# The square that the Newton step of a layer norm reads: from SBUF to PSUM, in a kernel whose order of work is a table

## The chip, the cores and the metric

The kernel runs on one core of a Trainium2 chip. Five engines of the core matter here, each with its own queue that it works through in order: TensorE (PE in the rows, with its weight loads as PEld), VectorE (DVE), ScalarE (ACT), GpSimd (POOL) and SyncE (SP, which here only starts transfers). The metric is the device time of one launch in microseconds (us): 888.38 us as the median of three runs (888.12 to 890.67).

## The reference

```python
# dynamic convolution: 7 taps, weights by token and head (softmax over the taps)
w = exp(weight_gen - max(weight_gen, -1)); w = w / (sum(w, -1) + 1e-9)     # (8, 4224, 8, 7)
y[b, s, h*24:(h+1)*24] = sum_k w[b, s, h, k] * x_pad[b, s + k, h*24:(h+1)*24]   # x: (8, 4224, 192)
# layer norm without a bias, two products with a relu between them, and the residual
xn = (y - mean(y)) / sqrt(var(y) + 1e-6) * g_ln
out = y + maximum(xn @ w_ch1, 0) @ w_ch2            # w_ch1: 192 x 768, w_ch2: 768 x 192
```

## The kernel before, in words

The 8 x 4224 tokens lie as 128 partitions of 264 tokens each. They are worked in 25 parts: three of 4 tokens per partition, twenty of 12, one of 8 and one of 4. A part's way through the engines:

- SP loads `x` into a ring and the tap weights `w`. The softmax goes over DVE (maximum L453, sum L469), POOL (L455, L473) and ACT; ACT writes the normalised tap weights of a chunk of 6 tokens into one of two PSUM banks, `wn` (L485).
- DVE multiplies `x` by the tap weights for seven taps, in four instructions per chunk (L522: three of 128x2304 into `pr` and one of 128x1152 into `y`). The products are added into `y` by POOL (L525) and by transfers that add, started from POOL (L528).
- ACT takes the mean and the variance of every token (L586, L591). Then follows, once per part, the reciprocal root for all of its tokens at once: on ACT `root` (a logarithm L613, an exponential L614 and the square of the result L615, all on rows of `s4` in SBUF), and on DVE `newton` (L618, twice L620, L622), four small instructions that sharpen the root by one Newton step. `newton` keeps two of its intermediate rows in the spare columns of a `wn` bank (`aux`), the bank that the last multiplication before it read.
- ACT scales the tokens (`xh`, L634) and rounds them to a high half in f16 (L703), POOL makes the low half (L705), and a transposing transfer puts both into `xT`. The first two groups of 4 tokens are transposed on TensorE instead (L657), and DVE makes their low half (`tlo`, L669).
- For each group of 4 tokens TensorE runs three units of the first product (L727, 36 instructions with weights loaded for each, into one of two `ph` buffers) and, for the group before, two halves of the second product (`p0`, `p1`, L778, 72 instructions each, into the single buffer `po`). A `ph` is evicted by ACT (relu to f16, `hh`, L742) and then by DVE (the rest that f16 lost, `hlo`, L744); `po` is scaled and added to `y` by DVE (L830), and SP writes `y` out.

The weights are prepared on the chip in the first 60 us, and four transfers swap halves of the first weight (`c_w`, L991) before the first unit can run through.

What sets the order: `PLACE` is a table that gives every operation a number; operations are recorded in the order of these numbers, and so each engine's queue has its order from them. Which buffer an operation gets follows from the same numbers. The semaphore waits are laid on afterwards, from the data and the buffers that two engines share.

Of the kernel before, what the change touches and what calls it, by code (L numbers as in the profile page):

```python
# [32 lines left out]
HALF = 512  # L33
# [4 lines left out]
    'wload': (2, 0, 19, 39, 47, 95, 111, 219, 239, 496, 460, 650, 902, 907, 911, 980, 1122, 1214, 1272, 1651, 1652,  # L38
        1484, 1705),
    'load': (3, 5, 1, 4, 7, 12, 62, 96, 160, 159, 94, 235, 320, 286, 417, 297, 369, 463, 499, 605, 707, 555, 758,  # L40
        798, 941, 843, 878, 914, 1126, 1053, 1211, 1175, 1338, 1174, 1295, 1380, 1379, 1449, 1634, 1576, 1571, 1797,
        1853, 1841, 1773, 1908, 1951, 2065, 2172),
    'w_load': (40, 28, 27),
    'w_gain': (50, 11, 45),
    'w_load2': (41,),
    'w_as': (87,),
    'w_av': (92, 103, 106),
    'w_an': (109,),
    'w_cs': (70,),
    'w_cv': (74, 75, 78),  # L50
    'w_cn': (82,),
    'w_s1': (113, 117, 121, 126, 129),
    'w_d': (154, 137),
    'w_h': (145, 131),
    'w_l': (156, 138),
    'w_lc': (168, 150),
    'w_m': (176, 172, 180, 179),
    'w_c2s': (81, 142, 135),
    'w_c2v': (84, 86, 88, 148, 152, 155, 140, 143, 146),
    'w_c2n': (112, 162, 151),  # L60
    'w_s2': (164, 174, 182, 186, 209, 207, 216, 227),
    'max': (8, 6, 51, 89, 100, 295, 188, 391, 443, 564, 679, 685, 923, 924, 1100, 1109, 1193, 1306, 1373, 1675,
        1686, 1624, 1826),
    'sub': (10, 9, 54, 98, 127, 299, 197, 400, 513, 588, 731, 805, 929, 999, 1104, 1209, 1285, 1409, 1502, 1678,
        1701, 1790, 1960),
    'exp': (13, 14, 65, 105, 171, 311, 230, 426, 527, 607, 738, 853, 931, 1044, 1110, 1222, 1289, 1423, 1516, 1683,
        1716, 1803, 2002),
    'sum': (15, 17, 76, 108, 217, 316, 233, 471, 557, 697, 752, 861, 977, 1059, 1150, 1231, 1292, 1427, 1553, 1695,
        1720, 1886, 2014),
    'log': (16, 23, 90, 114, 229, 319, 395, 483, 580, 730, 781, 882, 1006, 1085, 1206, 1253, 1381, 1450, 1606, 1710,  # L70
        1801, 1913, 2043),
    'less': (18, 26, 93, 122, 264, 363, 431, 524, 585, 735, 801, 892, 1023, 1090, 1226, 1296, 1383, 1468, 1621,
        1713, 1888, 1933, 2045),
    'expw': (20, 21, 38, 43, 107, 99, 187, 169, 284, 282, 371, 390, 470, 457, 569, 570, 646, 660, 765, 767, 865,
        863, 963, 934, 1029, 1058, 1167, 1188, 1274, 1236, 1390, 1347, 1495, 1451, 1590, 1546, 1674, 1687, 1774, 1757,
        1894, 1927, 1969, 1980, 2100, 2076, 2161),
    'keep': (24, 22, 67),
    'c0': (25, 29, 60, 61, 110, 175, 193, 246, 321, 344, 404, 425, 509, 533, 574, 648, 690, 739, 792, 849, 875, 912,
        979, 1027, 1062, 1082, 1185, 1196, 1282, 1374, 1392, 1485, 1531, 1493, 1593, 1667, 1714, 1754, 1810, 1872, 1914,
        1958, 2000, 2041, 2127, 2101, 2194),  # L80
    'c1': (33, 37, 46, 69, 132, 158, 240, 203, 331, 296, 459, 414, 476, 548, 573, 615, 701, 760, 804, 836, 896, 932,
        990, 1050, 1093, 1134, 1197, 1239, 1301, 1342, 1442, 1408, 1524, 1541, 1645, 1655, 1692, 1741, 1849, 1868, 1902,
        1972, 2009, 2070, 2131, 2119, 2193),
    'c2': (32, 36, 42, 49, 128, 153, 211, 263, 298, 362, 374, 437, 508, 485, 610, 593, 674, 732, 814, 770, 867, 952,
        1007, 1001, 1124, 1114, 1219, 1246, 1327, 1348, 1419, 1474, 1512, 1568, 1602, 1639, 1737, 1693, 1844, 1822,
        1946, 1928, 2024, 1985, 2136, 2152, 2181),
# [996 lines left out]
```

## Time and profile before

| | |
|---|---|
| median of three runs | 888.38 us |
| the profiled execution | 893.53 us, of which its span (first to last instruction) 891.8 us |
| mean granted TensorE clock | 0.977 |
| busy: TensorE / DVE / POOL / ACT | 831.6 / 768.1 / 697.2 / 686.7 us |
| `newton`'s first instruction (L618), all 25 | 38.1 us |

How to read it: engine busy time is a share of the span, and an engine that is idle costs only where something later waits for it. The rows below are from the profiled execution alone, which is 5.15 us above the median of the runs that were timed. A row of a timeline gives the start, the length, the instruction, and in brackets how long the engine had stood idle before it and which instruction released it.

### The profile page before, as it was taken

How to read it: one execution, taken by the hardware profiler on the slowest of the kernel's cores; microseconds unless marked ns; L12 is line 12 of the kernel's file. 1: busy time of each engine (PE TensorE's matmuls, PEld its weight loads, DVE VectorE, ACT ScalarE, POOL GpSimd, SP SyncE). 2: the span in 40 equal slices, each digit the busy share in tenths (PEclk: the TensorE clock that was granted, in tenths of full speed). 3: DMA queues.
4: the chain of work that ended last, by engine and by line, in shares of the span. 5: the costliest groups of instructions: out<-in, count | busy, mean ns of one | idle time of the engine just before them, and what ended most of it. 6: DMA issues, size and time to landing. Idle time of an engine off the chain costs nothing. (4 is left out here: it accounts for less than half of the span.)

```text
span 891.8 us, 37250 instructions
## 1 busy us (share of the span) xinstructions
PE 831.6 (93%) x16687; PEld 811.5 (91%) x16687; DVE 768.1 (86%) x646; ACT 686.7 (77%) x1797; POOL 697.2 (78%) x385
## 2 busy tenths in 40 slices
PE   5557999999899999999999998989998989999998
PEld 5347999999899999999999998989998989999997
DVE  6999999999999989999998898999898987874433
ACT  3888899798797887996888968876885869868621
POOL 4898899999889989978988879887886868874100
PEclk9869999999999999999999999999998999999999
DMA  8778687888697997886878887697896756554332
GB/s 237 182 169 173 137 186 168 189 175 164 151 183 154 236 205 151 165 191 147 187 187 183 164 158 160 137 180 145 196 183 124 133 119 136 134 114 96 74 65 81
DMA packets 132157, 140.86 MB, mean 158 GB/s; under 512 B 104102, under 2 KB 106030, under 8 KB 131998
## 3 DMA queue, kind: packets, MB, share of 16 engines
q1 hardware_dynamic: 119326, 88.16, 44.1%
q0 software_dynamic: 12672, 50.34, 29.0%
q8 instruction: 130, 2.13, 1.0%
q14 instruction: 29, 0.24, 0.1%
HBM read 36.43 MB, written 25.95 MB: 70 GB/s over the span
## 5 line engine op out<-in xcount | busy, mean ns | idle before, releaser
L525 POOL TENSOR_TENSOR y<-y,pr 128x1152 f32<-128x1152 f32 (+1 forms) x176 | 469.5, 2675 | 38.0 <-DVE pr L522 17.4
L727 PE MATMUL ph<-xT,c_w 64*128 64x256 f16 x7128 | 420.8, 271 | 20.9 <-DVE hlo L744 14.5
L727 PEld LDWEIGHTS <-c_w 64*128 64x128 f16 x7128 | 388.2, 95 | 29.3 <-issue 23.9
L778 PE MATMUL po<-c_w2h,hh 64*128 64x192 f16 x3120 | 391.8, 244 | 12.6 <-DVE y L830 10.5
L778 PE MATMUL po<-c_w2h,hlo 64*128 64x192 f16 x3120 | 391.6, 244 | 0.1
L778 PE MATMUL po<-c_w2l,hh 64*128 64x192 f16 x3120 | 391.6, 244 | 0.0
L522 DVE TENSOR_TENSOR pr<-x,wn 128x2304 f32<-128x2304 f32 (+2 forms) x138 | 332.2, 2417 | 6.6 <-POOL y L525 2.4
L778 PEld LDWEIGHTS <-hh 64*128 64x128 f16 x6240 | 318.8, 95 | 15.5 <-issue 13.8
L744 DVE SCALAR_TENSOR_TENSOR hlo<-ph,hh 128x1024 f16<-128x1024 f32 x198 | 239.1, 1218 | 86.1 <-ACT hh L742 85.7
L742 ACT ACTIVATE hh<-ph 128x1024 f16<-128x1024 f32 x198 | 199.0, 1012 | 102.6 <-PE ph L727 83.9
L778 PEld LDWEIGHTS <-hlo 64*128 64x128 f16 x3120 | 187.3, 95 | 0.3 <-issue 0.3
L634 ACT ACTIVATE xh<-y,s 128x192 f32<-128x192 f32 x264 | 126.6, 536 | 33.9 <-DVE s L622 31.6
L705 POOL TENSOR_TENSOR hl<-xh,hl 128x768 f16<-128x768 f32 x64 | 109.1, 1714 | 49.9 <-ACT hl L703 34.9
L591 ACT ACTIVATE junk<-y,s 128x192 f32<-128x192 f32 x264 | 119.4, 452 | 9.4 <-PE po L778 3.0
L528 POOL DMA_DIRECT2D pr<-pr x88 | 80.9, 961 | 53.0 <-DVE pr L522 30.2
L586 ACT ACTIVATE junk<-y 128x192 f32<-128x192 f32 x264 | 95.0, 360 | 20.0 <-POOL y L525 9.1
L830 DVE SCALAR_TENSOR_TENSOR y<-po,c_fs,y 128x768 f32<-128x768 f32 (+1 forms) x86 | 68.7, 813 | 4.0 <-PE po L778 4.0
L522 DVE TENSOR_TENSOR y<-x,wn 128x1152 f32<-128x1152 f32 (+2 forms) x47 | 59.5, 1268 | 2.2 <-ACT wn L485 2.2
L703 ACT ACTIVATE hl<-xh 128x768 f16<-128x768 f32 x64 | 53.2, 835 | 2.1 <-PE po L778 1.5
L586 ACT ACTIVATION_READ_ACCUMULATOR junk<-y 128x1 f32 x264 | 49.5, 187 | 0.0
L591 ACT ACTIVATION_READ_ACCUMULATOR junk<-y,s 128x1 f32 x264 | 49.5, 187 | 0.0
L618 DVE SCALAR_TENSOR_TENSOR wn<-s 128x12 f32<-128x12 f32 (+2 forms) x25 | 38.1, 1523 | 8.6 <-ACT s L615 8.3
(77 smaller groups left out, 319.0 us busy)
## 6 DMA issues: line engine op xcount, KB each, us to landing
pr<-pr POOLq DMA_DIRECT2D x80, 576.0 KB, 6.6
x<-in_x_dram SPq DMA_DIRECT2D x40, 576.0 KB, 6.1
out_dram<-y SPq DMA_DIRECT2D x40, 576.0 KB, 5.6
w<-in_weight_gen_dram SPq DMA_DIRECT2D x21, 336.0 KB, 5.8
pr<-pr POOLq DMA_DIRECT2D x8, 384.0 KB, 5.1
x<-in_x_dram SPq DMA_DIRECT2D x5, 384.0 KB, 5.2
out_dram<-y SPq DMA_DIRECT2D x4, 384.0 KB, 4.5
x<-in_moe_w_ch_dram SPq DMA_DIRECT2D x1, 1152.0 KB, 13.0
```

The costliest lines, as they stand in the source:

```text
L522: E.tensor_tensor(out=ov, in0=xv, in1=wv, op=ALU.mult)
L525: Q.tensor_tensor(out=flat(0), in0=flat(0), in1=flat(k), op=ALU.add)
L528: return Q.dma_start(flat(to), flat(k), accum_op=ALU.add, max_dma_last_dim=CHUNK * D * 4)
L586: A.activation(junk, at(y)[:, j, :], AF.Identity, scale=-SQ / D, accum_out=at(s4)[:, 3, t : t + 1])
L591: A.activation(junk, at(y)[:, j, :], AF.Square, scale=SQ, bias=at(s4)[:, 3, t : t + 1], accum_out=at(s4)[:, 0, t : t + 1])
L634: A.activation(paired(xh, t), at(y)[:, i, :].rearrange("p (c q) -> p c q", q=P // 2), AF.Identity, bias=at(s4)[:, 3, g + t : g + t + 1], s ...
L705: lambda xh=xh, hl=hl: Q.tensor_tensor(out=halves(hl, True), in0=pairs(xh), in1=halves(hl, False), op=ALU.subtract),
L727: T_.matmul(ph[:, r, v * 2 * P : (v + 1) * 2 * P], W["w1"][rows, WB[r][c], w, f : f + P], xv[rows, a, c, :, :], start=(v == 0 and k == 0), ...
L742: lambda: A.activation(at(hh)[:, us, :], at(ph), AF.Relu), [ph], [(hh, u)])
L744: lambda: V.scalar_tensor_tensor(out=at(hlo)[:, us, :], in0=at(ph), scalar=0.0, in1=at(hh)[:, us, :], op0=ALU.max, op1=ALU.subtract),
L778: made.append(T_.matmul(at(po)[:, z, e * D : (e + 1) * D], token(b, 2 * z + e, j)[rows], W[w][rows, j, :], start=(ph == 0 and e == 0 and k ...
L830: V.scalar_tensor_tensor(out=ysl, in0=at(po)[:, zs[0] : zs[-1] + 1, : 2 * D], scalar=W["fs"][:, 0:1], in1=ysl, op0=ALU.mult, op1=ALU.add)
```

## The change

ACT's `root` writes the square of the root into a third spare row of the `wn` bank (PSUM) in place of a row of `s4` (SBUF), and `newton`'s first instruction reads it there. So that instruction has one input in SBUF (the variance, `row(0)`) and one in PSUM. The bank is fixed when `root` is recorded, in `mine`. Both operations name a common key, `"aux"`, so that the `root` of a part is placed after the `newton` of the part before. The numbers of `PLACE` are new for all operations; two lines of the table show it. Because of three added lines, a line of this part of the code has a number higher by 3 in the changed kernel: `root`'s square is L618 there, and `newton` L621, L623 and L625.

```diff
 PLACE = {
-    'newton': (97, 141, 183, 258, 358, 466, 559, 664, 757, 855, 961, 1073, 1160, 1279, 1384, 1472, 1580, 1681, 1802,
+    'newton': (97, 159, 190, 254, 362, 464, 564, 669, 757, 857, 961, 1076, 1161, 1282, 1383, 1473, 1581, 1679, 1800,
...
-    assert AUX + 2 * PMAX <= HALF
+    assert AUX + 3 * PMAX <= HALF
...
         def aux(i):
-            return plan.pools["wn"][bank[0]][:, AUX + i * PMAX : AUX + i * PMAX + n]
+            return plan.pools["wn"][mine[0]][:, AUX + i * PMAX : AUX + i * PMAX + n]
+
+        mine = [0]
 
         def root():
+            mine[0] = bank[0]
             A.activation(row(1), row(0), AF.Ln, bias=bias[:, 0:1])
             A.activation(row(1), row(1), AF.Exp, scale=-0.5)
-            A.activation(row(2), row(1), AF.Square)
+            A.activation(aux(2), row(1), AF.Square)
 
         def newton():
-            V.scalar_tensor_tensor(out=aux(0), in0=row(0), scalar=EPS, in1=row(2), op0=ALU.add, op1=ALU.mult)
+            V.scalar_tensor_tensor(out=aux(0), in0=row(0), scalar=EPS, in1=aux(2), op0=ALU.add, op1=ALU.mult)
...
-        op("ACT", 670, ("rstd", S0), root, vs, [(s4, "r")])
-        op("V", 780, ("newton", S0), newton, [*vs, (s4, "r")], [(s4, "n"), *ms])
+        op("ACT", 670, ("rstd", S0), root, vs, [(s4, "r"), "aux"])
+        op("V", 780, ("newton", S0), newton, [*vs, (s4, "r"), "aux"], [(s4, "n"), *ms])
```

What the new table does to the queues is shown at three places. The first is DVE's queue around the twentieth `newton` of the program's twenty-five (the one at 668.51 us in the trace of before); the row that reads `po_106` is the addition of the second product (L830 before, L833 after), the `hlo` rows are evictions. In before:

```order
L744 SCALAR_TENSOR_TENSOR hlo_90<-ph_105,hh_88 128x1024 [waits Activation_49]
L744 SCALAR_TENSOR_TENSOR hlo_90<-ph_104,hh_88 128x1024 [waits Activation_49]
L469 TENSOR_REDUCE sm_94<-w_66 128x96
L618 SCALAR_TENSOR_TENSOR wn_103<-s_99 128x12 [waits DVE_49,Activation_49]
L620 SCALAR_TENSOR_TENSOR wn_103<-wn_103,s_99 128x12 [waits DVE_49]
L620 SCALAR_TENSOR_TENSOR s_99<-wn_103,s_99 128x12 [waits DVE_49]
L622 SCALAR_TENSOR_TENSOR s_99<-wn_103,s_99 128x12
L830 SCALAR_TENSOR_TENSOR y_74<-po_106,c_fs,y_74 128x768 [waits PE_49]
```

And in the change:

```order
L747 SCALAR_TENSOR_TENSOR hlo_90<-ph_104,hh_88 128x1024 [waits Activation_49]
L747 SCALAR_TENSOR_TENSOR hlo_90<-ph_105,hh_88 128x1024 [waits Activation_49]
L469 TENSOR_REDUCE sm_94<-w_66 128x96
L833 SCALAR_TENSOR_TENSOR y_72<-po_106,c_fs,y_72 128x768 [waits PE_49]
L621 SCALAR_TENSOR_TENSOR wn_103<-s_99,wn_103 128x12 [waits Activation_49]
L623 SCALAR_TENSOR_TENSOR wn_103<-wn_103,s_99 128x12 [waits DVE_49]
L623 SCALAR_TENSOR_TENSOR s_99<-wn_103,s_99 128x12 [waits DVE_49]
L625 SCALAR_TENSOR_TENSOR s_99<-wn_103,s_99 128x12
```

The first Newton instruction now names `wn_103` among its inputs, and the addition of the second product moved ahead of `newton`. Elsewhere on DVE most operations keep their rank among DVE's or move by one.

The second place is ACT's queue around the twentieth `root`: the logarithm, the exponential and the square, then the scaling `xh` that waits for DVE's `newton`, the tap weights `wn` of a later chunk, and evictions `hh`. In before:

```order
L591 ACTIVATE junk_101,s_99<-y_75,s_99 128x192 [waits Activation_49] x2
L613 ACTIVATE s_99<-s_99,bias 128x12 [waits Activation_49]
L614 ACTIVATE s_99<-s_99 128x12 [waits Activation_49]
L615 ACTIVATE s_99<-s_99 128x12 [waits Activation_49]
L634 ACTIVATE xh_81<-y_72,s_99 128x3x64 [waits DVE_49,Pool_49]
L634 ACTIVATE xh_81<-y_72,s_99 128x3x64
L485 ACTIVATE wn_102<-e_96 128x336 [waits Pool_49]
L742 ACTIVATE hh_89<-ph_104 128x1024 [waits PE_49]
```

And in the change:

```order
L591 ACTIVATE junk_101,s_99<-y_74,s_99 128x192 [waits Activation_49] x2
L616 ACTIVATE s_99<-s_99,bias 128x12 [waits Activation_49]
L617 ACTIVATE s_99<-s_99 128x12 [waits Activation_49]
L618 ACTIVATE wn_103<-s_99 128x12 [waits DVE_49,Activation_49]
L485 ACTIVATE wn_102<-e_97 128x336 [waits Pool_49]
L637 ACTIVATE xh_82<-y_68,s_99 128x3x64 [waits DVE_49]
L637 ACTIVATE xh_82<-y_68,s_99 128x3x64
L745 ACTIVATE hh_89<-ph_105 128x1024 [waits PE_49]
```

The square has a new wait for DVE, for the multiplication before it that read the bank; 20 of the 25 squares have it. `wn` moved ahead of `xh`.

The third place is DVE's queue at the start, ahead of the first eviction: `xT_85` and `xT_86` are the low halves of the first two groups (`tlo`, L669 before, L672 after), which the first units of TensorE need, and the 128x2304 rows are multiplications. In before:

```order
L522 TENSOR_TENSOR pr_80<-x,wn_102 128x2304 [waits DMAHW5_49,Pool_49]
L522 TENSOR_TENSOR pr_76<-x,wn_102 128x2304 [waits Activation_49]
L927 TENSOR_SCALAR c_r_126<-po_106 128x1 [waits PE_49]
L522 TENSOR_TENSOR pr_77<-x,wn_102 128x2304 [waits DMASW2_49,Pool_49]
L618 SCALAR_TENSOR_TENSOR wn_102<-s_100 128x4 [waits DVE_49,Activation_49]
...
L453 TENSOR_REDUCE mx_93<-w_65 128x96 [waits DMAHW6_49]
L669 TENSOR_TENSOR xT_85<-ph_104,xT_85 128x2x384
L522 TENSOR_TENSOR pr_78<-x,wn_102 128x2304 [waits DMAHW0_49,Activation_49]
L669 TENSOR_TENSOR xT_86<-ph_105,xT_86 128x2x384 [waits Activation_49]
```

And in the change:

```order
L672 TENSOR_TENSOR xT_85<-ph_104,xT_85 128x2x384 [waits PE_49]
L522 TENSOR_TENSOR pr_80<-x,wn_102 128x2304 [waits DMAHW3_49,Pool_49]
L522 TENSOR_TENSOR pr_78<-x,wn_102 128x2304 [waits Activation_49]
L522 TENSOR_TENSOR pr_76<-x,wn_102 128x2304 [waits DMASW2_49,Pool_49]
L930 TENSOR_SCALAR c_r_126<-po_106 128x1 [waits PE_49]
L453 TENSOR_REDUCE mx_93<-w_65 128x96 [waits DMAHW6_49]
L621 SCALAR_TENSOR_TENSOR wn_102<-s_100,wn_102 128x4 [waits Activation_49]
L623 SCALAR_TENSOR_TENSOR wn_102<-wn_102,s_100 128x4 [waits DVE_49]
L623 SCALAR_TENSOR_TENSOR s_100<-wn_102,s_100 128x4 [waits DVE_49]
L625 SCALAR_TENSOR_TENSOR s_100<-wn_102,s_100 128x4
L672 TENSOR_TENSOR xT_86<-ph_104,xT_86 128x2x384 [waits PE_49]
```

The low half of the first group moved ahead of three multiplications, a maximum and a `newton`. TensorE's own queue has the same order of units and halves as before.

## Rows read from the trace of the kernel before

**Rows 1.** The page's first part: busy us, share, instructions by engine.
```profile
PE 831.6 (93%) x16687; PEld 811.5 (91%) x16687; DVE 768.1 (86%) x646; ACT 686.7 (77%) x1797; POOL 697.2 (78%) x385
```
**Rows 2.** Windows: stretch, length, busy by engine (PE to POOL), clock, DMA share, GB/s.
```profile
100.00:150.00 50.00, 48.51 (x1034) 48.18 (x1030) 49.52 (x38) 44.12 (x121) 47.85 (x27) 1.00 0.77 168
800.00:850.00 50.00, 50.00 (x1062) 49.84 (x1058) 21.94 (x28) 35.45 (x84) 16.50 (x10) 1.00 0.38 86
```
**Rows 3.** Timeline of PE, rows with an idle time: start, length, what, [idle <-releaser].
```profile
61.33 6.65 PE L727 MATMUL ph<-xT,c_w 64*128 64x256 f16 x72 [5.44 <-DVE xT L669]
...
89.98 3.37 PE L727 MATMUL ph<-xT,c_w 64*128 64x256 f16 x34 [3.51 <-DVE hlo L744]
...
231.36 0.26 PE L778 MATMUL po<-c_w2h,hh 64*128 64x192 f16 x2 [2.58 <-DVE y L830]
...
602.14 3.74 PE L727 MATMUL ph<-xT,c_w 64*128 64x256 f16 x36 [2.19 <-DVE hlo L744]
...
676.36 0.34 PE L778 MATMUL po<-c_w2h,hh 64*128 64x192 f16 x2 [4.24 <-DVE y L830]
...
717.29 0.26 PE L778 MATMUL po<-c_w2h,hh 64*128 64x192 f16 x2 [3.02 <-DVE y L830]
```
**Rows 4.** Waits: who waited for whom, us in total, times, longest.
```profile
PE ph L727 <- DVE hlo L744: 14.5, 17, 3.5
...
DVE wn L618 <- ACT s L615: 8.3, 11, 1.9
```
**Rows 5.** Timeline of DVE, the first Newton instruction ahead of these idle times.
```profile
84.49 3.81 DVE L618 SCALAR_TENSOR_TENSOR wn<-s 128x12 f32<-128x12 f32 x1 [0.22 <-ACT s L615]
...
226.21 3.68 DVE L618 SCALAR_TENSOR_TENSOR wn<-s 128x12 f32<-128x12 f32 x1
...
589.87 3.29 DVE L618 SCALAR_TENSOR_TENSOR wn<-s 128x12 f32<-128x12 f32 x1
...
668.51 6.37 DVE L618 SCALAR_TENSOR_TENSOR wn<-s 128x12 f32<-128x12 f32 x1
...
711.59 4.22 DVE L618 SCALAR_TENSOR_TENSOR wn<-s 128x12 f32<-128x12 f32 x1 [0.51 <-ACT s L615]
```
**Rows 6.** Lines L618 and L620: ns min/median/max, first and last start, forms.
```profile
L618 DVE SCALAR_TENSOR_TENSOR wn<-s x25: 169/1054/6373, 31.1 to 826.7; 128x12 f32<-128x12 f32 x20, 128x4 f32<-128x4 f32 x4, 128x8 f32<-128x8 f32 x1
...
L620 DVE SCALAR_TENSOR_TENSOR wn<-wn,s x25: 170/178/179, 32.0 to 826.9; 128x12 f32<-128x12 f32 x20, 128x4 f32<-128x4 f32 x4, 128x8 f32<-128x8 f32 x1
```
**Rows 7.** Timeline of POOL beside the Newton instruction of 668.51.
```profile
669.35 8.19 POOL L525 TENSOR_TENSOR y<-y,pr 128x1152 f32<-128x1152 f32 x3
```
**Rows 8.** The page's costliest groups: busy us, mean ns | idle before, releaser.
```profile
L525 POOL TENSOR_TENSOR y<-y,pr 128x1152 f32<-128x1152 f32 (+1 forms) x176 | 469.5, 2675 | 38.0 <-DVE pr L522 17.4
...
L618 DVE SCALAR_TENSOR_TENSOR wn<-s 128x12 f32<-128x12 f32 (+2 forms) x25 | 38.1, 1523 | 8.6 <-ACT s L615 8.3
```
**Rows 9.** Windows that begin where TensorE resumes after four of the idle times.
```profile
89.98:95.00 5.02, 5.02 (x70) 4.60 (x71) 5.02 (x5) 4.99 (x9) 3.35 (x2) 0.66 0.24 63
602.14:607.00 4.86, 4.86 (x66) 4.46 (x67) 4.33 (x4) 2.67 (x6) 2.56 (x4) 0.65 0.83 182
676.36:682.00 5.64, 5.64 (x81) 5.64 (x82) 5.17 (x3) 2.33 (x8) 1.18 (x1) 0.59 0.79 137
717.29:723.00 5.71, 5.71 (x93) 5.71 (x94) 5.71 (x4) 4.25 (x8) 2.05 (x2) 0.70 0.33 65
```
**Rows 10.** Lines by form on DVE: busy us, mean ns | idle before, releasers.
```profile
L522 DVE TENSOR_TENSOR pr<-x,wn 128x2304 f32<-128x2304 f32 x120 | 304.4, 2544 | 4.0 <-POOL y L525 2.4 <-issue 1.1 <-ACT wn L485 0.5
```
**Rows 11.** Timeline of SP: issue of the four swaps of the first weight.
```profile
54.26 2.50 SPq L991 DMA_DIRECT2D c_w<-c_w  x4
```
**Rows 12.** DMA issues: queue, count, KB each, median us from issue to landing.
```profile
c_w<-c_w SPq DMA_DIRECT2D x2, 192.0 KB, 5.4
```
**Rows 13.** Line L615 on ACT: ns min/median/max, first and last start, forms.
```profile
L615 ACT ACTIVATE s<-s x25: 205/212/213, 30.9 to 826.5; 128x12 f32<-128x12 f32 x20, 128x4 f32<-128x4 f32 x4, 128x8 f32<-128x8 f32 x1
```
**Rows 14.** Timeline of ACT: the square at 477.36.
```profile
477.36 0.21 ACT L615 ACTIVATE s<-s 128x12 f32<-128x12 f32 x1
```
**Rows 15.** Timeline of DVE: the last multiplication before that square's Newton step.
```profile
477.14 2.54 DVE L522 TENSOR_TENSOR pr<-x,wn 128x2304 f32<-128x2304 f32 x1
```

More of the change, by code (lines that the diff above doesn't have):

```diff
@@ L37 @@
 PLACE = {
[L38 to L86, printed above, removed]
@@ L102 @@
-    'squares': (83, 63, 125, 133, 178, 170, 222, 206, 225, 247, 251, 252, 325, 351, 352, 338, 333, 346, 403, 428,
[6 rows of a table removed]
-    'rstd': (91, 136, 181, 255, 356, 455, 556, 661, 753, 851, 959, 1069, 1159, 1266, 1371, 1469, 1578, 1665, 1800,
-        1885, 1990, 2073, 2180, 2272, 2266),
-    'newton': (97, 141, 183, 258, 358, 466, 559, 664, 757, 855, 961, 1073, 1160, 1279, 1384, 1472, 1580, 1681, 1802,
[9 rows of a table removed]
-    'thi': (139, 196),
-    'tlo': (191, 200),
[26 rows of a table removed]
-    'turn': (231, 279, 291, 315, 385, 412, 401, 491, 534, 540, 599, 640, 645, 703, 747, 751, 794, 832, 837, 901,
-        919, 936, 1025, 1049, 1033, 1115, 1161, 1166, 1205, 1260, 1265, 1334, 1367, 1376, 1437, 1430, 1475, 1527, 1523,
-        1595, 1630, 1647, 1704, 1743, 1749, 1788, 1838, 1851, 1903, 1934, 1943, 1977, 2032, 2064, 2098, 2114, 2169,
-        2163, 2217, 2253, 2237, 2284, 2316, 2329),
@@ L153 @@
-    'halo': (287, 436, 756, 1000, 1313, 1615, 2097),
-    'unit': (194, 204, 214, 223, 228, 242, 259, 268, 285, 303, 308, 323, 335, 342, 355, 372, 377, 392, 407, 415,
[10 rows of a table removed]
-    'relu': (201, 212, 220, 232, 243, 256, 275, 277, 294, 318, 313, 328, 357, 348, 361, 378, 384, 399, 416, 421,
[10 rows of a table removed]
-    'hlo': (208, 218, 224, 238, 253, 262, 278, 281, 304, 329, 317, 337, 368, 349, 367, 387, 405, 409, 423, 435, 448,
[14 rows of a table removed]
-    'hop': (248, 288, 326, 359, 393, 432, 468, 503, 542, 578, 612, 649, 686, 715, 755, 787, 819, 854, 891, 926, 962,
[16 rows of a table removed]
+    'wload': (1, 0, 29, 45, 63, 98, 114, 221, 241, 498, 419, 650, 901, 902, 905, 981, 1121, 1216, 1270, 1648, 1650,
+        1479, 1737),
@@ new lines @@
+    'load': (2, 10, 4, 3, 11, 12, 62, 64, 165, 171, 99, 244, 325, 295, 420, 306, 371, 467, 501, 607, 710, 557, 754,
+        801, 940, 846, 882, 913, 1128, 1054, 1217, 1178, 1344, 1176, 1301, 1387, 1381, 1448, 1636, 1588, 1575, 1801,
+        1849, 1847, 1776, 1907, 1945, 1962, 2115),
+    'w_load': (30, 31, 28),
+    'w_gain': (32, 27, 46),
+    'w_load2': (33,),
+    'w_as': (68,),
+    'w_av': (81, 93, 94),
+    'w_an': (104,),
+    'w_cs': (59,),
+    'w_cv': (73, 79, 80),
+    'w_cn': (106,),
@@ new lines @@
+    'w_s1': (113, 123, 126, 131, 137),
+    'w_d': (149, 143),
+    'w_h': (144, 142),
+    'w_l': (152, 146),
+    'w_lc': (163, 150),
+    'w_m': (167, 168, 162, 169),
+    'w_c2s': (72, 120, 105),
+    'w_c2v': (89, 91, 92, 153, 157, 160, 124, 134, 135),
+    'w_c2n': (103, 164, 156),
+    'w_s2': (170, 182, 188, 193, 201, 202, 209, 232),
+    'max': (5, 6, 55, 90, 109, 286, 189, 388, 447, 570, 679, 684, 921, 922, 1098, 1100, 1193, 1311, 1360, 1670,
+        1689, 1624, 1971),
+    'sub': (7, 8, 74, 96, 129, 300, 195, 400, 509, 587, 726, 792, 931, 998, 1104, 1210, 1280, 1410, 1496, 1678,
+        1700, 1786, 1982),
@@ new lines @@
+    'exp': (9, 19, 77, 107, 179, 309, 215, 426, 531, 602, 740, 854, 935, 1051, 1114, 1222, 1292, 1422, 1516, 1682,
+        1711, 1805, 2007),
+    'sum': (13, 22, 82, 112, 220, 316, 235, 470, 556, 697, 753, 859, 977, 1058, 1153, 1233, 1297, 1427, 1553, 1701,
+        1722, 1885, 2010),
+    'log': (14, 23, 84, 115, 228, 320, 394, 485, 580, 729, 782, 884, 1009, 1089, 1206, 1258, 1379, 1452, 1600, 1709,
+        1807, 1915, 2071),
+    'less': (15, 24, 95, 128, 269, 354, 429, 525, 593, 737, 805, 894, 1019, 1095, 1225, 1285, 1388, 1464, 1616,
+        1715, 1884, 1944, 2085),
@@ new lines @@
+    'expw': (16, 18, 43, 44, 101, 102, 187, 174, 276, 279, 360, 387, 465, 459, 569, 566, 648, 658, 767, 770, 865,
+        864, 962, 939, 1027, 1055, 1160, 1185, 1273, 1238, 1386, 1347, 1490, 1453, 1585, 1548, 1675, 1685, 1773, 1758,
+        1889, 1926, 1968, 1977, 2095, 2113, 2170),
+    'keep': (17, 20, 70),
+    'c0': (21, 35, 51, 56, 122, 180, 204, 252, 327, 347, 401, 428, 510, 537, 585, 653, 691, 743, 796, 852, 880, 917,
+        985, 1028, 1067, 1086, 1187, 1201, 1288, 1374, 1394, 1486, 1534, 1500, 1593, 1669, 1719, 1756, 1813, 1875, 1918,
+        1960, 2003, 2046, 2117, 2122, 2179),
@@ new lines @@
+    'c1': (36, 40, 57, 58, 133, 181, 239, 207, 330, 288, 451, 411, 474, 544, 572, 620, 700, 758, 803, 834, 898, 929,
+        988, 1046, 1092, 1132, 1200, 1236, 1300, 1340, 1435, 1402, 1522, 1538, 1634, 1657, 1691, 1743, 1843, 1864, 1901,
+        1969, 2009, 2054, 2157, 2168, 2187),
+    'c2': (34, 37, 52, 53, 111, 125, 219, 266, 298, 364, 376, 438, 505, 489, 617, 598, 671, 735, 814, 776, 868, 955,
+        1002, 1004, 1120, 1117, 1220, 1251, 1326, 1353, 1420, 1477, 1512, 1570, 1602, 1635, 1741, 1707, 1842, 1823,
+        1946, 1931, 2025, 1986, 2147, 2139, 2209),
@@ new lines @@
+    'c3': (25, 26, 83, 54, 132, 172, 234, 273, 313, 351, 383, 440, 527, 490, 605, 633, 660, 713, 787, 821, 891, 946,
+        1017, 1036, 1145, 1164, 1227, 1256, 1322, 1267, 1405, 1462, 1509, 1557, 1623, 1608, 1731, 1767, 1781, 1827,
+        1897, 1936, 2040, 2090, 2138, 2133, 2202),
+    'z0': (38, 39, 66),
+    'z1': (47, 41, 78),
+    'z2': (48, 42, 88),
+    'z3': (50, 49, 100),
+    'copy': (67, 60, 108),
+    'sums': (71, 69, 127, 117, 140, 139, 214, 185, 184, 227, 245, 226, 302, 296, 305, 334, 335, 338, 396, 417, 408,
[6 rows of a table added]
@@ new lines @@
+    'squares': (86, 85, 136, 138, 154, 155, 223, 197, 229, 230, 248, 246, 314, 345, 352, 339, 337, 349, 407, 425,
[6 rows of a table added]
+    'rstd': (87, 148, 178, 249, 356, 461, 560, 663, 756, 851, 960, 1075, 1159, 1272, 1373, 1471, 1578, 1667, 1798,
+        1888, 1991, 2077, 2181, 2258, 2286),
+    'newton': (97, 159, 190, 254, 362, 464, 564, 669, 757, 857, 961, 1076, 1161, 1282, 1383, 1473, 1581, 1679, 1800,
[9 rows of a table added]
+    'thi': (141, 186),
+    'tlo': (161, 192),
[26 rows of a table added]
+    'turn': (238, 292, 294, 322, 380, 415, 403, 496, 541, 545, 599, 641, 649, 705, 745, 748, 793, 830, 835, 890,
+        920, 934, 1026, 1049, 1033, 1115, 1167, 1171, 1209, 1260, 1263, 1336, 1368, 1377, 1438, 1433, 1474, 1528, 1526,
+        1580, 1629, 1647, 1699, 1738, 1746, 1790, 1834, 1838, 1898, 1932, 1942, 1975, 2034, 2067, 2097, 2114, 2154,
+        2156, 2223, 2254, 2237, 2298, 2299, 2329),
@@ new lines @@
+    'halo': (280, 435, 760, 999, 1310, 1611, 2042),
+    'unit': (191, 203, 210, 222, 231, 243, 259, 265, 287, 301, 304, 319, 336, 343, 353, 370, 375, 391, 406, 414,
[10 rows of a table added]
+    'relu': (199, 208, 212, 225, 257, 250, 271, 275, 291, 311, 317, 329, 342, 358, 365, 378, 389, 399, 416, 422,
[10 rows of a table added]
+    'hlo': (205, 218, 224, 237, 262, 255, 285, 284, 297, 315, 328, 331, 350, 367, 368, 384, 402, 410, 423, 431, 446,
[14 rows of a table added]
+    'hop': (247, 282, 318, 357, 393, 434, 462, 503, 538, 576, 612, 646, 682, 716, 755, 786, 816, 853, 889, 928, 958,
[16 rows of a table added]
```

9 lines of the change are left out of this document (removed), and 194 rows, old and new, of the table PLACE.

## The prediction

> **What bounds the kernel now.** I read the page's engine shares first, then the windows, TensorE's idle times, and what stood on DVE before each. TensorE is busy 831.6 us of 891.8, DVE 768.1, POOL 697.2 [rows 1]; in the stretch from 100 to 150 us TensorE, DVE and POOL are all above 95%, and DVE is the fullest with 49.52 of 50; from 800 to 850 us only TensorE is full [rows 2]. So TensorE sets the time, and DVE, which feeds it, sets it where TensorE stops. TensorE's order is untouched, so the change can pay in three ways: an earlier first unit, fewer stops, and less time at the lower clock after a stop. The reader is to see in [rows 3] where TensorE starts, 61.33 us, and five later stops of 2.19 to 4.24 us, each released by a DVE eviction or addition.
>
> In front of each of the five, DVE stood in one instruction, the first of `newton` [rows 5]. It has 12 elements per partition. The next instruction of the same size, L620, takes 170 to 179 ns at all 25 places; this one takes 169 to 6373 [rows 6], 38.1 us in 25 [rows 8]. The two differ in their inputs: L620 reads one row of PSUM and one of SBUF, L618 two of SBUF. During the longest, 668.51 to 674.88, POOL ran three additions back to back from 669.35 [rows 7], each some 2.67 us [rows 8]; the instruction ended about where the second did (669.35 + 2 x 2.73 = 674.81). So I read the excess as DVE waiting, inside the instruction, for POOL to let go of SBUF. The multiplications, one input in SBUF and one in PSUM, run in 2544 ns in the mean of 120 with POOL busy all along [rows 10], and DVE's full rate is near that, so this mix of inputs does not wait.
>
> **The change part by part.** *The first Newton instruction.* With one input in PSUM it becomes what L620 is: 25 x 0.175 = 4.4 us instead of 38.1, which takes 33.7 us from DVE. Most of that lies beside TensorE's work. On the path are the five stops [rows 3]. In each the stall is longer than the stop (3.81 against 3.51, 3.68 against 2.58, 3.29 against 2.19, 6.37 against 4.24, 4.22 against 3.02 [rows 3, 5]), so without it what TensorE waited for is there in time. Idle: 3.51 + 2.58 + 2.19 + 4.24 + 3.02 = 15.54 us.
>
> After four of the five, TensorE resumed at the lower of its two clocks for a while: over the windows that begin there the granted clock is 0.66, 0.65, 0.59 and 0.70 of 2.4 GHz [rows 9]. TensorE is busy throughout them, so each loses its length times what is missing: 5.02 x 0.34 = 1.71, 4.86 x 0.35 = 1.70, 5.64 x 0.41 = 2.31, 5.71 x 0.30 = 1.71, together 7.43 us. After the stop of 2.58 no such window stands. Without the stop the fall goes too. Together 22.97 us: 7.80 early (89.98 and 231.36) and 15.17 late.
>
> What is late next? In the early stretch POOL has 47.85 of 50 and DVE, less its stalls, is still nearly full [rows 2], so TensorE, coming earlier, will find other evictions late: between none and all is given back, and I take 60% as kept, 4.7 us, nearer the upper end because the relieved engine is the fullest. Late, the others have room, and I take 85%, 12.9 us. The other twenty stalls, 38.1 - 21.4 - 20 x 0.175 = 13.2 us, are not in front of a long stop, but DVE comes earlier by them, and TensorE waits for evictions in 14.5 us [rows 4], 8.8 without the stops of 3.51 and 2.19; of these I take a quarter, 2.2 us (bounds 0 and 8.8).
>
> *The square.* ACT's instruction took 205 to 213 ns into SBUF [rows 13]; into PSUM no row shows it. Between nothing and double it is 0 to 5 us of ACT over the kernel, and ACT is idle for 23% [rows 1]; I take no change. New is its wait: 20 of 25 squares wait for a DVE multiplication that read the bank. Queued behind it on ACT are evictions, tap weights and the scaling; TensorE and DVE wait for these. In the times of before, DVE had been at `newton` first at 11 of the 25 [rows 4], so at most 14 squares would be held, the longest that I find by 477.14 + 2.54 - 477.36 = 2.32 us [rows 14, 15]. Bounds: 0 and 14 x 2.32 = 32.5 us of ACT. ACT's idle time covers most of it, and DVE loses some tenths where it then waits for the square. I charge 1.5 us.
>
> *The order.* Most operations move by a place or none, so I give the steady part nothing of its own. At the twentieth `newton` the addition of the second product now stands ahead of it; the stop of 4.24 us would go by that alone, and it is counted once. TensorE was done there at 676.36 - 4.24 = 672.12 [rows 3], so `newton` behind the addition would start some 1 us later, still before the 674.88 at which its first instruction ended. At the start the low half of the first group moves ahead of three multiplications, 7.6 us by [rows 10], and was what released the first unit, after 5.44 us of idle [rows 3]. But the four weight swaps are issued from 54.26 to 56.76 [rows 11] and land some 5.4 us later [rows 12], from 59.7 to 62.2: they are late next, and hide most of the gain. Bounds 0 and 5.4; I take 2.0.
>
> *The sum.* 2.0 + 4.7 + 12.9 + 2.2 - 1.5 = 20.3 us. Against the profiled execution's own 893.53 (its span 891.8 and 1.7 around it) that is 873.2; the median of the runs is 5.15 below the profiled one, so 868.1: **868 us**, 2.3% less.
>
> **The rivals.** *All of it is gained* (0.17). If nothing is given back and the first unit starts as early as TensorE's idle there allows, the gain is 22.97 + 5.4 + 2.2 = 30.6, to about 858. For it: the stalls cover the stops whole. Against: TensorE then has to find every other producer in time.
>
> *DVE's time was not the limit* (0.14 in all). POOL's additions, 469.5 us [rows 8] in an engine above 95% early [rows 2], pace the convolution, and the stops come back elsewhere. If the late terms are halved and the early lost, the gain is 7.6, 881; if everything is lost, 888 within 2.7. That the instruction still waits, because it reads one row of SBUF, belongs here; L620's 179 ns at most speaks against it. Of the 0.14, 0.07 is for 881 and 0.07 for no change.
>
> *ScalarE held at the square* (0.06), the slower side. Place: the 20 squares that wait for a multiplication. If 14 are held by 2.32 us with an eviction behind them that TensorE is waiting for, 32.5 us come onto the path; less 22.97 and 2.0 gained, that is 7.5 us slower, 896. It decides from an average hold that reaches TensorE of some 25 / 14 = 1.8 us. Against it: at 11 places DVE was there first, and mostly an eviction or an addition stands on DVE between the multiplication and `newton`, so the square need not be early.
>
> The Trainium skill's page "PSUM — Partial Sum Buffer", section "PSUM bank collisions raise a hardware error", speaks for this rival: the hardware does not put off one engine's access to a bank that another is using, so program order must keep engines apart by bank, whatever the columns. By that rule every square waits for the whole multiplication before it, also where the columns differ, as the added waits in the order show. By the rule alone, an estimate would be 25 x 2.54 = 64 us of ACT; the times of before leave room for half of that. No trace of before has the square in PSUM.
>
> **How the numbers follow.** The forecast, 860 to 877, has 0.63; all of it 0.17; DVE not the limit 0.14; held at the square 0.06. What a measurement of this kernel can tell from no change is 0.3%, 2.7 us, so 885.7 to 891.1 is "same". Faster: 0.63 + 0.17 + 0.07 = 0.87; same 0.07; slower 0.06. The range runs from 857 (nearly everything kept) to 885 (a small part).
>
> **What would show it.** Right: the first Newton instruction at 0.17 to 0.2 us at all 25 places; DVE busy near 735 us; no stop of TensorE above 2 us released by an addition right behind a `newton`; fewer falls of the clock; the first unit at 58 to 60 us. Wrong: that instruction still above 0.3 us anywhere; waits of ACT's square for DVE of more than 10 us in all with idle TensorE behind them; or TensorE's idle time past 100 us as large as now, with POOL or transfers as the releaser.

## The result and the profile after

The changed kernel takes 864.7 us (median of 4 runs, 864.1 to 865.3) where the kernel before took 888.3 beside it (887.8 to 890.7): a ratio of 0.973, 95% interval 0.971 to 0.975, 23.6 us less. The profiled execution of the changed kernel took 864.73 us, at its median; that of before took 893.53, 5.3 above its own. So a comparison of the two traces has some 5 us more in it than the medians. Of all the runs that follow, one, of the new table alone at 889.7 us, was a slow one and is in no range or ratio.

The page's first part answers to [rows 1]: DVE's busy time went from 768.1 to 734.1 us, TensorE's from 831.6 to 821.8, for the same instructions. The line of the granted clock (tenths of 2.4 GHz, 40 slices) has no digit under 9 behind the third slice. Each slice is over 21 us long, and the four short stretches of before at 0.59 to 0.70 [rows 9] show in its own line as a single 8 (behind the third slice), so the windows further down, where the changed kernel has 1.00 from 100 us on, are the better evidence.

```profile
PE 821.8 (95%) x16687; PEld 792.2 (92%) x16687; DVE 734.1 (85%) x646; ACT 685.5 (79%) x1797; POOL 695.9 (81%) x385
...
PEclk9759999999999999999999999999999999999999
```

The first Newton instruction is L621 now, the square L618, and the lines behind it stand three further than before. Three answers on single lines (minimum, median and maximum in ns, first and last start) answer to [rows 6, 13]:

```profile
L621 DVE SCALAR_TENSOR_TENSOR wn<-s,wn x25: 156/166/176, 31.4 to 806.4; 128x12 f32<-128x12 f32 x20, 128x4 f32<-128x4 f32 x4, 128x8 f32<-128x8 f32 x1
...
L618 ACT ACTIVATE wn<-s x25: 177/183/184, 30.5 to 806.2; 128x12 f32<-128x12 f32 x20, 128x4 f32<-128x4 f32 x4, 128x8 f32<-128x8 f32 x1
...
  DVE pr L522: 1.8, 3
...
  DVE pr L522: 9.1, 4
  DVE wn L621: 7.4, 7
```

At none of 25 places does the instruction take over 176 ns; it was up to 6373. The last three lines are the square's waits (in all, and at how many places): ScalarE idled 1.8 us in 3 for DVE ahead of it, and DVE waited for the square 9.1 us with a multiplication and 7.4 with `newton`.

TensorE's timeline, its rows with an idle time of over 1.2 us from the first unit on, answers to [rows 3]:

```profile
59.96 3.42 PE L730 MATMUL ph<-xT,c_w 64*128 64x256 f16 x36
65.02 1.25 PE L730 MATMUL ph<-xT,c_w 64*128 64x256 f16 x19 [1.64 <-DVE c_r L940]
...
69.05 2.14 PE L730 MATMUL ph<-xT,c_w 64*128 64x256 f16 x36 [1.89 <-DVE hlo L747]
...
72.65 2.14 PE L730 MATMUL ph<-xT,c_w 64*128 64x256 f16 x36 [1.45 <-DVE hlo L747]
...
293.13 2.14 PE L730 MATMUL ph<-xT,c_w 64*128 64x256 f16 x36 [1.45 <-DVE hlo L747]
```

The first row is the first unit (it has no idle time of its own); behind 73 us a single stop of that size is left, where there were six. Where the time went is best seen in windows over the same stretches of both traces, before first, then after (stretch, length, then busy us and number of instructions of PE, PEld, DVE, ACT and POOL, granted clock, DMA share, GB/s):

```profile
0.00:100.00 100.00, 66.91 (x703) 56.15 (x705) 89.90 (x98) 73.70 (x208) 77.08 (x52) 0.86 0.79 183
100.00:300.00 200.00, 193.77 (x4088) 191.51 (x4084) 193.04 (x153) 171.10 (x459) 185.36 (x100) 1.00 0.81 174
300.00:500.00 200.00, 196.81 (x4166) 195.35 (x4163) 185.47 (x149) 168.36 (x439) 178.11 (x96) 1.00 0.84 177
500.00:700.00 200.00, 189.87 (x3926) 185.15 (x3922) 180.47 (x139) 151.74 (x398) 160.77 (x86) 0.97 0.80 162
700.00:850.00 150.00, 146.89 (x3082) 146.34 (x3078) 105.22 (x97) 113.77 (x288) 95.90 (x55) 0.99 0.54 113
```

And the changed kernel:

```profile
0.00:100.00 100.00, 68.13 (x759) 57.25 (x761) 86.29 (x100) 75.90 (x215) 78.32 (x54) 0.85 0.76 179
100.00:300.00 200.00, 196.70 (x4150) 194.39 (x4147) 189.09 (x156) 172.07 (x459) 188.99 (x101) 1.00 0.85 183
300.00:500.00 200.00, 199.14 (x4227) 189.81 (x4224) 182.83 (x151) 171.85 (x458) 182.22 (x99) 1.00 0.84 179
500.00:700.00 200.00, 199.94 (x4264) 193.38 (x4260) 184.84 (x153) 165.22 (x426) 173.21 (x94) 1.00 0.79 173
700.00:850.00 150.00, 149.90 (x3196) 149.74 (x3191) 87.65 (x87) 100.42 (x242) 73.15 (x42) 1.00 0.45 100
```

TensorE's order is the same in both, so its instruction counts measure progress, at about 21 per us. The changed kernel gets further by 56, 62, 61, 338 and 114 instructions: some 2.7, 3.0, 2.9, 15.9 and 5.4 us, 29.9 together, where the spans differ by 29.4 (both traces have the same 16687 matrix instructions on record). Seven tenths lies behind 500 us. Nothing comes from the first 80 us, where the changed kernel falls behind:

```profile
0.00:80.00 80.00, 50.75 (x401) 40.90 (x403) 70.19 (x83) 57.51 (x170) 61.41 (x44) 0.85 0.81 192
...
0.00:80.00 80.00, 49.27 (x362) 38.70 (x364) 66.46 (x82) 56.31 (x167) 58.40 (x43) 0.81 0.75 181
```

At 80 us it has done 39 instructions less (362 for 401; 351 in its second trace), and between 80 and 100 us, where the kernel before has its stop at 89.98 [rows 3], it wins 95. From 100 to 850 us TensorE was idle 22.7 us of 750 before and 4.3 after.

### The profile page after: what moved, and what is told of

It is laid out like the page before. It is cut to its first block, busy times and chain, and to the rows that moved or that the text cites. A ratio compares the mean times of both kernels' runs of the same rounds, so it can differ in the third digit from the quotient of the medians.

```text
span 862.4 us, 37233 instructions
## 1 busy us (share of the span) xinstructions
PE 821.8 (95%) x16687; PEld 792.2 (92%) x16687; DVE 734.1 (85%) x646; ACT 685.5 (79%) x1797; POOL 695.9 (81%) x385
## 3 DMA queue, kind: packets, MB, share of 16 engines
q0 software_dynamic: 12672, 50.34, 29.9%
## 5 line engine op out<-in xcount | busy, mean ns | idle before, releaser
L525 POOL TENSOR_TENSOR y<-y,pr 128x1152 f32<-128x1152 f32 (+1 forms) x176 | 476.3, 2724 | 26.1 <-DVE pr L522 10.2
L730 PE MATMUL ph<-xT,c_w 64*128 64x256 f16 x7128 | 414.2, 270 | 10.4 <-DVE hlo L747 8.4
L730 PEld LDWEIGHTS <-c_w 64*128 64x128 f16 x7128 | 371.6, 94 | 28.9 <-issue 13.3
L781 PE MATMUL po<-c_w2l,hh 64*128 64x192 f16 x3120 | 386.4, 243 | 0.5 <-issue 0.5
L781 PE MATMUL po<-c_w2h,hh 64*128 64x192 f16 x3120 | 386.2, 243 | 0.5 <-DVE y L833 0.5
L781 PE MATMUL po<-c_w2h,hlo 64*128 64x192 f16 x3120 | 386.2, 243 | 0.0
L781 PEld LDWEIGHTS <-hh 64*128 64x128 f16 x6240 | 300.7, 94 | 2.3 <-issue 0.8
L781 PEld LDWEIGHTS <-hlo 64*128 64x128 f16 x3120 | 169.2, 94 | 0.7 <-issue 0.7
L708 POOL TENSOR_TENSOR hl<-xh,hl 128x768 f16<-128x768 f32 x64 | 113.7, 1794 | 54.9 <-ACT hl L706 51.5
L528 POOL DMA_DIRECT2D pr<-pr x88 | 83.2, 983 | 27.8 <-DVE pr L522 20.3
L833 DVE SCALAR_TENSOR_TENSOR y<-po,c_fs,y 128x768 f32<-128x768 f32 (+1 forms) x86 | 68.6, 815 | 6.0 <-PE po L781 5.9
L586 ACT ACTIVATION_READ_ACCUMULATOR junk<-y 128x1 f32 x264 | 49.5, 187 | 0.0
L473 POOL TENSOR_TENSOR e<-e,sm 128x672 f32<-128x672 f32 (+2 forms) x23 | 35.5, 1543 | 5.6 <-ACT sm L471 5.6
```

The lines of the kernel that those rows point to most:

```text
L525: Q.tensor_tensor(out=flat(0), in0=flat(0), in1=flat(k), op=ALU.add)
L528: return Q.dma_start(flat(to), flat(k), accum_op=ALU.add, max_dma_last_dim=CHUNK * D * 4)
L586: A.activation(junk, at(y)[:, j, :], AF.Identity, scale=-SQ / D, accum_out=at(s4)[:, 3, t : t + 1])
L708: lambda xh=xh, hl=hl: Q.tensor_tensor(out=halves(hl, True), in0=pairs(xh), in1=halves(hl, False), op=ALU.subtract),
L730: T_.matmul(ph[:, r, v * 2 * P : (v + 1) * 2 * P], W["w1"][rows, WB[r][c], w, f : f + P], xv[rows, a, c, :, :], start=(v == 0 and k == 0), ...
L781: made.append(T_.matmul(at(po)[:, z, e * D : (e + 1) * D], token(b, 2 * z + e, j)[rows], W[w][rows, j, :], start=(ph == 0 and e == 0 and k ...
```

## The experiments

Two theories stood against each other. Theory 1: the stall of the instruction that reads two SBUF rows beside GpSimd's work accounts for the gain. The rival: the new table of places does. A third, open in the prediction, was that GpSimd's own pace limits the kernel.

**The edit under the old table**

```diff
-            A.activation(row(2), row(1), AF.Square)
+            A.activation(aux(2), row(1), AF.Square)
...
-            V.scalar_tensor_tensor(out=aux(0), in0=row(0), scalar=EPS, in1=row(2), op0=ALU.add, op1=ALU.mult)
+            V.scalar_tensor_tensor(out=aux(0), in0=row(0), scalar=EPS, in1=aux(2), op0=ALU.add, op1=ALU.mult)
```

> The table of before, the square written to PSUM and read from there (one key that orders two norms at the very end is left out, so that the old table can stand). Theory 1, the stall of the first Newton instruction cost the time: the instruction takes 0.16 to 0.2 us at all 25 places, DVE is busy some 735 us, the five long stops are gone, and the time is 863 to 870 us. Rival, the new order made the gain: the instruction is short here too, but the time stays at 884 to 889. Rival, both are needed: 873 to 882.

Measured: 865.6 us (864.8 to 866.3), ratio 0.974 (0.971 to 0.977). The edit alone gives what the whole change gives, within 0.9 us. The first Newton instruction's range is 156 to 176 ns, and the first unit starts at 59.02 us, 2.3 earlier than before [rows 3], with the old order of the start:

```profile
59.02 3.38 PE L730 MATMUL ph<-xT,c_w 64*128 64x256 f16 x30 [3.62 <-DVE xT L672]
```

**The new table alone**, the square in SBUF as before.

> The new table alone, the square in SBUF as before. Theory 1: the first Newton instruction is again long, 30 to 45 us in 25, stops of TensorE of 2 to 5 us stand right behind it, and the time is 883 to 893. Rival, the new order made the gain: 863 to 870 with the stalls still there. Rival, both are needed: 873 to 882.

Measured: 879.8 us (876.3 to 886.8, 9 runs), ratio 0.991 (0.988 to 0.994). Theory 1 had 883 to 893 here and missed. By the number this is the third expectation, but the run ahead of it rules out that both are needed: with the stalls there, the table gives some 9 us; with the stalls gone it gives 0.9 (865.6 against 864.7, and the two ranges overlap). The runs lie in two groups, six at 876 to 880 us and three at 885 to 887, and only one of the second, 885.5 us, has a trace. In it the instruction takes 35.2 us in 25 (busy us, mean ns | idle before it):

```profile
L618 DVE SCALAR_TENSOR_TENSOR wn<-s 128x12 f32<-128x12 f32 (+2 forms) x25 | 35.2, 1409 | 9.1 <-ACT s L615 7.0 <-ACT wn L485 1.6
```

Its timeline of TensorE has the first unit where it was before [rows 3], and stops of 1.5 to 6.05 us at other places; the longest comes behind a stall of 5.89 us at 327.47:

```profile
61.28 4.94 PE L727 MATMUL ph<-xT,c_w 64*128 64x256 f16 x68
...
337.51 2.74 PE L727 MATMUL ph<-xT,c_w 64*128 64x256 f16 x24 [6.05 <-DVE hlo L744]
...
742.86 3.73 PE L727 MATMUL ph<-xT,c_w 64*128 64x256 f16 x36 [3.04 <-DVE hlo L744]
```

So a table decides where the stalls fall, and it seems how much of them reaches TensorE. Which of its lines saves the 9 us, and how the stalls lie in the faster runs, is not settled.

**The old read put back**: one instruction more ahead of `newton`, in the changed kernel.

```diff
         def newton():
+            V.scalar_tensor_tensor(out=aux(0), in0=row(0), scalar=EPS, in1=row(1), op0=ALU.add, op1=ALU.mult)
             V.scalar_tensor_tensor(out=aux(0), in0=row(0), scalar=EPS, in1=aux(2), op0=ALU.add, op1=ALU.mult)
```

> The changed kernel, with one DVE instruction more ahead of each newton: of the form that the change took out (12 elements, two rows of SBUF as inputs, result into the PSUM row that the next instruction overwrites). The output is the same. Theory 1, the time goes where DVE reads two SBUF rows beside a working POOL: the added instruction takes 20 to 45 us in 25, the one behind it stays at 0.16 to 0.2, and the time comes back to 878 to 892. Rival, the order or the place of the square made the gain: the added instruction takes 0.17 us at each place and the time is 864 to 867.

Measured: 886.2 us (885.4 to 887.9, 10 runs), ratio 0.997 (0.995 to 0.998). Its two instructions stand side by side, first the one with two SBUF inputs, then the one with one:

```profile
L621 DVE SCALAR_TENSOR_TENSOR wn<-s 128x12 f32<-128x12 f32 (+2 forms) x25 | 30.8, 1233 | 8.0 <-ACT wn L618 6.8 <-ACT wn L485 1.1
...
L622 DVE SCALAR_TENSOR_TENSOR wn<-s,wn 128x12 f32<-128x12 f32 (+2 forms) x25 | 4.3, 173 | 0.9
```

The order and the place of the square are those of the changed kernel, its waits are nearly so (DVE's multiplications wait for it 7.3 us in 4), and 21.5 of the 23.6 us are lost again. That falls to theory 1.

**Who holds DVE.** The kernel before, with GpSimd's 176 additions cut to 12 elements.

```diff
-            Q.tensor_tensor(out=flat(0), in0=flat(0), in1=flat(k), op=ALU.add)
+            Q.tensor_tensor(out=flat(0)[:, :12], in0=flat(0)[:, :12], in1=flat(k)[:, :12], op=ALU.add)
```

> The kernel before, with GpSimd's additions of the taps (176 of 2.7 us) cut to the first 12 of their 384 to 1152 elements, so that the sums are left incomplete. Nothing of DVE, of the order or of the square's place is changed. Theory 1, DVE stands in the first Newton instruction because GpSimd works in SBUF: the 38.1 us of that instruction fall to under 12 (what is left stands beside GpSimd's other operations), the five long stops go, and the time is 860 to 870 us. Rival, it waits for something else (ScalarE's result, a transfer): it stays at 25 to 45 us. Rival, GpSimd paces the kernel apart from the stall: the time falls under 858.

Measured: 864.2 us (862.1 and 866.4), ratio 0.972 (0.966 to 0.978). The two-SBUF read is still in the code, GpSimd is busy for 33%, and DVE's instruction falls from 38.1 [rows 8] to 10.5 us:

```profile
PE 821.1 (95%) x16687; PEld 800.8 (93%) x16687; DVE 740.3 (86%) x646; ACT 685.8 (80%) x1797; POOL 286.1 (33%) x385
...
L618 DVE SCALAR_TENSOR_TENSOR wn<-s 128x12 f32<-128x12 f32 (+2 forms) x25 | 10.5, 421 | 8.5 <-ACT s L615 8.2
```

The time is the changed kernel's, and behind 67 us no stop of over 1.2 us is left in the trace. So it was GpSimd's work that held the instruction, and GpSimd's pace costs nothing beyond that: with 410 us less work the kernel gains no more than by the edit.

**The instruction twice**, in the kernel before.

```diff
             V.scalar_tensor_tensor(out=aux(0), in0=row(0), scalar=EPS, in1=row(2), op0=ALU.add, op1=ALU.mult)
+            V.scalar_tensor_tensor(out=aux(0), in0=row(0), scalar=EPS, in1=row(2), op0=ALU.add, op1=ALU.mult)
```

> The kernel before, with the first Newton instruction issued twice (same inputs, same result). If DVE hands the way back to GpSimd after each instruction, the second one waits as well: the two take 50 to 80 us in 50, and the time is 893 to 905. If DVE, once it has it, keeps it for the next: the second takes 0.17 us at each place, 42 us in all, and the time is 888 to 892.

Measured: 914.2 us (909.2 to 919.5), ratio 1.028 (1.022 to 1.034), slower than either expected. The second instruction, right behind the first, waits as well, but only at some places:

```profile
L618 DVE SCALAR_TENSOR_TENSOR wn<-s 128x12 f32<-128x12 f32 (+2 forms) x25 | 30.6, 1223 | 8.5 <-ACT s L615 8.2
...
L619 DVE SCALAR_TENSOR_TENSOR wn<-s 128x12 f32<-128x12 f32 (+2 forms) x25 | 26.6, 1065 | 0.9
...
L619 DVE SCALAR_TENSOR_TENSOR wn<-s x25: 170/178/6044, 32.8 to 853.0; 128x12 f32<-128x12 f32 x20, 128x4 f32<-128x4 f32 x4, 128x8 f32<-128x8 f32 x1
...
458.78 0.67 DVE L618 SCALAR_TENSOR_TENSOR wn<-s 128x12 f32<-128x12 f32 x1
459.48 6.04 DVE L619 SCALAR_TENSOR_TENSOR wn<-s 128x12 f32<-128x12 f32 x1
...
692.24 6.37 DVE L618 SCALAR_TENSOR_TENSOR wn<-s 128x12 f32<-128x12 f32 x1
698.65 0.18 DVE L619 SCALAR_TENSOR_TENSOR wn<-s 128x12 f32<-128x12 f32 x1
```

Its median is 178 ns: at 18 of 25 places it runs through, behind each first instruction of over 1.2 us among them. At seven places it takes 1.29 to 6.04 us, at five of these behind a first one of 0.67 us or less. So neither expectation holds at all places.

Together 57.2 us in place of 38.1. Beside the changed kernel (4.2 us in that instruction) 53 us of stall cost 49.5; in the kernel before, 33.9 cost 23.6. By these medians a microsecond of stall costs about 0.7 to 0.9 us of the whole time, TensorE's lower clock behind a stop included. The stalls are those of the profiled executions, though, and by the times of these (919.5, 893.5 and 864.7 us) it is 0.85 to 1.03.

**One input in place of two on GpSimd**, in the kernel before: the additions are replaced by a scaling, so that the sums are incomplete.

```diff
-            Q.tensor_tensor(out=flat(0), in0=flat(0), in1=flat(k), op=ALU.add)
+            Q.tensor_scalar(out=flat(0), in0=flat(k), scalar1=1.0, scalar2=None, op0=ALU.mult)
```

> The kernel before, with GpSimd's additions of the taps replaced by a scaling by 1.0 of the product alone into the same output (one SBUF input in place of two), so that the sums are left incomplete. If only GpSimd's two-input operations hold DVE: its first Newton instruction falls under 12 us in 25 and the time is 860 to 872. If any GpSimd operation in SBUF holds it: 20 to 40 us remain, in proportion to what the scaling takes beside the additions' 2.7 us, and stops remain behind it.

Measured: 932.7 us (932.1 and 933.3), ratio 1.049 (1.043 to 1.055). The scaling takes longer than the addition did, and DVE's instruction 56.3 us (51.8, 4.3 and 0.2 in its three sizes), more than expected:

```profile
L618 DVE SCALAR_TENSOR_TENSOR wn<-s 128x12 f32<-128x12 f32 x20 | 51.8, 2588 | 4.6 <-ACT s L615 4.4
...
L618 DVE SCALAR_TENSOR_TENSOR wn<-s 128x4 f32<-128x4 f32 x4 | 4.3, 1078 | 1.1 <-ACT s L615 1.0
```

One SBUF input on GpSimd's side is enough to hold DVE; its second input is not the cause. How much of the 932.7 us is the slower scaling itself was not separated.

**The new wait.** At the start of the changed kernel DVE stands for 4.38 us ahead of a multiplication, because the square writes into the bank that it reads, and stands behind four `xh` in ScalarE's queue (the square is at 57.50, the multiplication at 57.71):

```profile
50.78 2.54 DVE L522 TENSOR_TENSOR pr<-x,wn 128x2304 f32<-128x2304 f32 x1
57.71 5.02 DVE L522 TENSOR_TENSOR pr<-x,wn 128x2304 f32<-128x2304 f32 x2 [4.38 <-ACT wn L618]
```

The edit that prices it puts the square into the other bank:

```diff
-            mine[0] = bank[0]
+            mine[0] = 1 - bank[0]
```

> The changed kernel, with the square (and the two other PSUM rows of newton) in the other of the two tap-weight banks than the one whose taps DVE multiplied last. It prices the new wait of the change: DVE's multiplications waited for the square 9.1 us in 4 and its newton 7.4 us in 7 in the changed kernel. If that wait costs time: the multiplications' share falls under 3 us and the time is 860 to 863.5. If it costs nothing or comes back as a wait for the next taps: 864 to 868, the same as the changed kernel or a little more.

Measured: 862.7 us (862.3 to 863.5), ratio 0.970 (0.967 to 0.974). The multiplications' wait falls from 9.1 us in 4 to 2.7 in one:

```profile
DVE wn L621 <- ACT wn L618: 6.9, 7, 2.3
...
DVE pr L522 <- ACT wn L618: 2.7, 1, 2.7
```

Both kernels were run again side by side.

> The changed kernel once more, on the chip and beside the runs of the next one, so that the two can be compared directly: 864 to 866 us.

> The changed kernel with the square and newton's other PSUM rows in the other tap-weight bank, again, beside the changed kernel itself. If the first run's 2 us were real: 862 to 863.5 us, with no value of it above the lowest of the changed kernel. If they were the difference between two chips: the same as the changed kernel within 1 us.

Measured: the changed kernel 864.7 (864.2 to 865.2), the other bank 863.5 (862.8 to 865.9). The wait is as small as the first time, but one run lies above all of the changed kernel's, against the first expectation. A gain of 1 to 2 us is likely and not shown beyond doubt. Under the old table, where the multiplications waited 0.4 us for the square, the other bank should give nothing:

> The edit under the table of before, with the square in the other tap-weight bank. If the new table is worth nothing once the stall is gone, and the other bank saves the same 2 us here as under the new table: 862 to 865. If the old table already had no square in the way (DVE's multiplications waited for it 0.4 us there): 865 to 867.

Measured: 864.9 us (862.5 to 866.1), ratio 0.972 (0.967 to 0.977), at the border between the two expectations and not to be told from the edit alone (864.8 to 866.3).

## Why the prediction was right

**The instruction.** The 33.7 us of DVE came as forecast, 33.9: from 38.1 to 4.2 us, DVE busy 734.1 where some 735 was named. That GpSimd is what DVE waits for was read from one coincidence of times [rows 5, 7]; cutting GpSimd's additions shows it. That it takes two inputs in SBUF on DVE's side is shown by the two neighbours in one kernel, 30.8 against 4.3 us, where a second neighbour with two such inputs took 26.6. The Trainium skill's page "SBUF — State Buffer", section "Who interferes with whom", has the rule: a DVE instruction with two inputs in SBUF contends with a GpSimd instruction that reads SBUF; one with at most one input there does not, outside DVE's two-port modes. The rows agree on both halves: the two neighbours, and the 56.3 us beside a GpSimd instruction that reads one input.

**The five stops: mis-sized.** The step that failed is "what is late next". It kept 60% of the early and 85% of the late term and a quarter of the other waits, 4.7 + 12.9 + 2.2 = 19.8 us, since TensorE, coming earlier, would find other producers late. It found nearly none: from 100 us on, 4.3 us of idle are left, and the clock is 1.00 in every window. At 21 instructions per us the early term came nearly whole: 95 instructions between 80 and 100 us and 62 up to 300 are 4.5 and 3.0 us, of 7.8 in full. By the windows TensorE was busy 336.76 of the late 350 us (500 to 850) before and 349.84 after, 13.1 us more, and with the clock that is some 21 us of progress, where the late term in full was 15.2. What the late stretch has beyond that, 6 us, and the 2.9 between 300 and 500 are the smaller waits, put at 2.2. All this is from one execution of each kernel, that of before 5 us above its median. A full GpSimd, 47.85 of 50 us, was one of the two reasons to expect something late; with GpSimd at 33% the time is the same, so its high share was work spread over the time and no limit. For DVE's share no run tests it.

**The square's wait.** 1.5 us were charged with 0 to 32.5 as bounds. ScalarE was held 1.8 us in all, in 3 squares, as the low end had it. The wait came from the other side: DVE's multiplications waited for the square, 9.1 us, and the prediction gave that only "some tenths". By the other bank its price is some 1 to 2 us, not shown beyond doubt, so the size of the term fits, and its place was wrong.

**The start.** This term failed too. The first unit starts at 59.96 us, in the range named (58 to 60), but nothing is gained by it: at 80 us the changed kernel is 39 instructions behind, some 2 us, where 2.0 were to be won. With the old table and the edit the first unit starts at 59.02 (two of the stalls, 0.83 us at 31.11 and 1.19 at 45.33 in the trace of before, lie ahead of it, and the edit takes both), and at 80 us 451 instructions are done; with the new table alone it starts at 61.28. The prediction had the weight swaps late next; no wait of TensorE for them shows in the trace. The second unit waits until 65.02 for operations of DVE that stand behind the multiplication held for 4.38 us; with the square in the other bank, and without that wait, 409 instructions are done at 80 us.

**The order.** Nothing was given to the steady part for the table, and with the stalls gone the whole of it is worth 0.9 us, within the noise. That it is worth 9 us where the stalls are was not seen.

**The sum.** 20.3 us were forecast; the profiled executions differ by 28.8 and the medians by 23.6. That 868 came within 3.3 us is in part luck. Against the profiled execution's own time the forecast was 8.5 us short (873.2 for 864.73), and the start, which lost, made up for a part of what the stops gave beyond their terms. Then the forecast took the profiled execution's 5 us above the median off at the end, as if they had nothing to do with the change. They may have: the kernel before spreads from 885.9 to 892.8 over 19 runs, the changed one from 864.1 to 865.3 over 9. But one kernel with the stalls keeps within 2.6 us (the old read put back), and one nearly without them has its two runs 4.2 apart (the short additions), so what spreads the times stays open.

The rival of ScalarE held at the square, 896 us, fell with the 1.8 us; that DVE's time was not the limit fell with the late stretch; "all of it is gained" was right on the stops (next to nothing given back) and wrong on the start.
